# Expert blocks of a routed two-layer network: gathers three blocks ahead, two buffers each, first-layer weights split before the second layer

## The chip, the cores and the metric

The kernel runs on one core of one Trainium2 chip. The core has five engines that run side by side, each in the order of its own queue: TensorE (PE in the profile, with its weight loads as PEld), VectorE (DVE), ScalarE (ACT), GpSimd (POOL) and SyncE (SP, which here only issues DMAs). They wait for each other and for DMAs through semaphores. The metric is the device time of one execution in microseconds (us), given as the median of several runs.

## What is computed

The reference is an attention layer followed by a routed feed-forward network. Keys and values are averaged over groups of 8 positions (576 to 72), attention runs per batch (8) and head (8), and its output gives 8 x 576 = 4608 rows of 512 numbers. Each row then goes through one of 8 experts:

```python
logits = np.einsum('bsd,de->bse', x, w_gate)
local_gate = 1.0 / (1.0 + np.exp(-np.einsum('bsd,de->bse', x, w_local).squeeze(-1)))
...
        fresh_e = int(np.argmax(logits[b, s]))
        if s == 0 or local_gate[b, s] < 0.5:
            e = fresh_e
        else:
            e = prev_e if prev_e >= 0 else fresh_e
...
        h = np.maximum(x[b, s] @ w1[e], 0.0)
        out[b, s] = p[e] * (h @ w2[e])
```

Which expert a row uses is known only when the kernel has computed the logits. w1[e] is 512 x 1024 and w2[e] is 1024 x 512.

## The kernel before

The first part (attention, logits, choice of expert) writes the 4608 rows to a table in memory, `x_rows`, and for each expert a list of its rows. It ends in a small table `tab`, read with `entry`, that cuts the lists into **blocks** of up to 256 rows of one expert. A block with 128 rows or fewer is a **single** (`l1_one`), the others are **two-half blocks** (`l1_two`). Two plans written out by hand (`PLAN_B`, `PLAN_C`) set the order of the work up to block 0; then block 1 and the blocks from 2 on follow, the latter in `blocks(b)`, an unrolled chain of conditionals on registers.

Every product is made of three products with values split in a rounded upper part and its remainder: ScalarE writes the upper part, VectorE subtracts it from the original. So an expert's weights need four such pairs for w1 (`weights1`, `split1`, tiles w1h and w1l) and four for w2 (`weights2`, `split2`, w2h and w2l), from raw copies that SyncE has loaded, and each block's 256 rows need two (`x_split`). TensorE's first layer (lines 331 and 333) fills eight PSUM tiles one after the other; ScalarE and VectorE empty each with two operations apiece (lines 338, 339, 343, 344). Six PSUM tiles rotate there (hp, tp and rt). The second layer (line 352) makes the two output halves, half 1 first. `emit_scale` multiplies a half by its gate on VectorE into `ob`, and `emit_rows` scatters it to the output with an indirect DMA from GpSimd's queue.

In the kernel before, one block runs in this order: the first layer; `next_x`, which is the transposing of the next block's gathered rows (`x_turn`, line 319), the sums that give the list of rows to gather (`ids_sum`) and the two splits of the transposed rows; `fetch`, in which GpSimd issues eight indirect DMAs (`gather`, line 315) for the block after the next and SyncE loads another list; then `rest`: the second layer's half 1, its scaling and scatter, half 0, the splits of w1 and of w2 if the next block has another expert, and the scaling and scatter of half 0. There is one buffer each for the gathered rows (`xk`), the list (`idk`), the split rows (`xt`) and the outputs (`ob`). So that one DMA wait is taken at one place, GpSimd executes tiny operations that touch a buffer after its DMA: `seen_o` (line 1069) waits until the scatter from `ob` is done and then lets `emit_scale` write it; `seen_x` (line 1072) does the same for gathered rows; `emit_rows` copies its positions first (lines 1075 and 1076); `fetch` has two more (lines 1087 and 1088). `meta_shift` moves the positions and gates of three blocks along.

## Time and profile before

| | us |
|---|---|
| median of 3 runs (724.74 to 728.71) | 727.87 |
| profiled execution | 729.17 |
| its span, first to last instruction | 727.0 |
| blocks 1 to 20, TensorE (279.32 to 708.76) | 429.44 |
| from TensorE's last matmul to the end of the span | 18.24 |

Times in the rows are us from the start of the span. A timeline row gives start, duration, engine, line of the kernel, operation, destination and source; brackets give the idle time before it and what ended it. A name such as DVEq stands for an engine's instruction stream itself (a branch, say) and not for a computation. [...] Busy time is not progress: a matmul at half clock is busy for longer.

### The profile page before, as it was taken

What the parts mean: (1) busy time and instruction counts of PE and PEld (TensorE: products, weight loads), DVE (VectorE), ACT (ScalarE), POOL (GpSimd) and SP (SyncE); (2) the same over time, 40 slices, a digit from 0 to 9 for tenths busy, and PEclk for the clock granted to TensorE, in tenths of its full rate; (3) what the DMA queues carried; (4) which work ended last, traced back from release to release, by engine and by line L of the source; (5) the groups of instructions that cost most, each with busy time, mean ns of one, the idle gap of its engine ahead of it and who ended that gap; (6) DMA issues with size and microseconds to landing.
All of it is one profiled execution on the core that took longest, in us unless ns stands there. A gap on an engine that the chain in (4) does not pass through costs nothing. (4 is left out here: it accounts for less than half of the span.)

```text
span 727.0 us, 12051 instructions
## 1 busy us (share of the span) xinstructions
PE 633.5 (87%) x3588; PEld 534.7 (74%) x3588; DVE 454.3 (62%) x1061; ACT 273.1 (38%) x612; POOL 444.9 (61%) x652
## 2 busy tenths in 40 slices
PE   2868798787798999989999979799998996999990
PEld 1757687676686888778888768588877884888880
DVE  5557699887777743354569338478944486844450
ACT  1234354335354342232265126165622264422230
POOL 5165658675557543667556667676766766766553
PEclk9989899977679999999999989899999998899995
DMA  7988754744412127111117214426721136611111
GB/s 199 312 270 290 248 206 166 230 147 148 121 61 96 30 74 265 37 57 46 50 53 266 63 44 158 166 69 247 272 62 46 45 109 238 237 60 47 42 50 39
DMA packets 49443, 97.52 MB, mean 134 GB/s; under 512 B 22974, under 2 KB 22978, under 8 KB 49348
## 3 DMA queue, kind: packets, MB, share of 16 engines
q1 hardware_dynamic: 38820, 74.34, 30.6%
q0 software_dynamic: 10528, 22.08, 9.7%
q8 instruction: 39, 0.64, 0.4%
q14 instruction: 56, 0.46, 0.2%
HBM read 76.28 MB, written 22.21 MB: 135 GB/s over the span
## 5 line engine op out<-in xcount | busy, mean ns | idle before, releaser
L315 POOL DMA_INDIRECT kt<-x_rows,idk x168 | 185.1, 1102 | 48.8 <-issue 39.0
L331 PE MATMUL hp<-x,w1h 128*128 128x512 f32 x376 | 143.5, 419 | 7.4 <-ACT w1h L213 3.6
L352 PE MATMUL o_ps<-w2h,ht_h 128*128 128x512 f32 x312 | 122.6, 393 | 1.5 <-PEq L1141 1.5
L333 PE MATMUL hp<-x,w1l 128*128 128x256 f32 x376 | 111.1, 296 | 12.8 <-DVEq L1147 10.5
L352 PE MATMUL o_ps<-w2h,ht_l 128*128 128x512 f32 x312 | 121.7, 390 | 0.0
L352 PE MATMUL o_ps<-w2l,ht_h 128*128 128x512 f32 x312 | 121.6, 390 | 0.0
L331 PEld LDWEIGHTS hp<-x,w1h 128*128 128x128 f32 x376 | 75.4, 200 | 26.4 <-ACT w1h L213 4.1
L333 PEld LDWEIGHTS hp<-x,w1l 128*128 128x128 f32 x376 | 75.6, 201 | 17.3 <-DVEq L1147 12.3
L338 ACT COPY hs<-hp 128x256 f32<-128x256 f32 x94 | 34.8, 371 | 140.7 <-PE hp L333 140.5
L567 PE MATMUL op<-vaug,aT 128*128 128x148 f32 (+4 forms) x448 | 77.8, 340 | 2.1 <-ACT aT L377 1.8
L567 PEld LDWEIGHTS op<-vaug,aT 128*128 128x128 f32 (+1 forms) x448 | 69.4, 203 | 8.7 <-ACT aT L377 3.1
L339 DVE TENSOR_TENSOR hs<-hp,hs 128x256 f32<-128x256 f32 x94 | 39.4, 422 | 56.8 <-ACT hs L338 55.3
L352 PEld LDWEIGHTS o_ps<-w2h,ht_h 128*128 128x128 f32 x312 | 58.6, 188 | 14.7 <-ACT ht_h L966 2.5
L1066 DVE TENSOR_SCALAR ob<-o_ps,m_a 128x512 f32<-128x512 f32 x42 | 31.5, 749 | 59.3 <-PE o_ps L352 41.0
L343 ACT ACTIVATE ht_h<-hs 128x256 fp32r<-128x256 f32 x136 | 57.1, 420 | 30.1 <-DVE hs L339 30.1
L352 PEld LDWEIGHTS o_ps<-w2h,ht_l 128*128 128x128 f32 x312 | 58.5, 188 | 12.7
L352 PEld LDWEIGHTS o_ps<-w2l,ht_h 128*128 128x128 f32 x312 | 58.6, 188 | 11.5
L344 DVE SCALAR_TENSOR_TENSOR ht_l<-hs,ht_h 128x256 fp32r<-128x256 f32 x136 | 58.7, 432 | 5.9 <-ACT ht_h L343 5.8
L1077 POOL DMA_INDIRECT out<-ob,m_e x42 | 44.3, 1054 | 25.8 <-issue 25.8
L1069 POOL TENSOR_TENSOR ob<-zf 128x1 f32<-128x1 f32 x61 | 19.1, 313 | 54.0 <-DMA out<-ob,m_e 53.6
L383 POOL TENSOR_TENSOR t<-vt_in 128x512 f32<-128x512 f32 (+1 forms) x22 | 24.9, 1132 | 39.8 <-DMA vt_in<-in_v 39.4
L377 ACT COPY osb<-op 128x444 f32<-128x444 f32 (+2 forms) x56 | 26.5, 477 | 52.6 <-PE op L567 47.2
(261 smaller groups left out, 1184.2 us busy)
## 6 DMA issues: line engine op xcount, KB each, us to landing
raw<-in_moe_w SPq DMA_DIRECT2D x56, 512.0 KB
kk<-in_k SPq DMA_DIRECT2D x16, 576.0 KB
vt_in<-in_v SPq DMA_DIRECT2D x16, 512.0 KB
qt<-in_q SPq DMA_DIRECT2D x16, 512.0 KB
x_rows<-xs SPq DMA_DIRECT2D x16, 512.0 KB
kt<-x_rows,idk POOLq DMA_INDIRECT x168, 2.6
vt_in<-in_v SPq DMA_DIRECT2D x8, 256.0 KB
vt_in<-in_moe_w SPq DMA_DIRECT2D x4, 512.0 KB
```

What stands on the lines that cost most here:

```text
L315: nc.gpsimd.indirect_dma_start(out=xk[:, j, :], out_offset=None, in_=x_pc[0:4 * rows], in_offset=bass.IndirectOffsetOnAxis(ap=idk[:, j:j + ...
L331: nc.tensor.matmul(out=ps, lhsT=W1[0][:, kk, f * P:(f + 1) * P], rhs=xt[:, kk].rearrange("p i n -> p (i n)"), start=(kk == 0), stop=False, ...
L333: nc.tensor.matmul(out=ps[:, 0:2 * P], lhsT=W1[1][:, kk, f * P:(f + 1) * P], rhs=xt[:, kk, 0, :], start=False, stop=(kk == KD - 1), skip_g ...
L338: nc.scalar.copy(out=hb[:, 0, :], in_=ps[:, 2 * P:])
L339: nc.vector.tensor_tensor(out=hb[:, 1, :], in0=ps[:, 0:2 * P], in1=hb[:, 0, :], op=ALU.add)
L343: nc.scalar.activation(out=ht[0][:, f, :], in_=hb, func=AF.Relu)
L344: nc.vector.scalar_tensor_tensor(out=ht[1][:, f, :], in0=hb, scalar=0.0, in1=ht[0][:, f, :].bitcast(F32), op0=ALU.max, op1=ALU.subtract)
L352: nc.tensor.matmul(out=to[h], lhsT=ht[i][:, kk, h * P:(h + 1) * P], rhs=W2[j][:, kk, :], start=(n == 0), stop=(n == 3 * KF - 1))
L377: nc.scalar.copy(out=out, in_=in_)
L567: nc.tensor.matmul(out=out, lhsT=lhs, rhs=rhs if len(out.shape) == 3 else rhs.rearrange("p s x -> p (s x)"), start=all(x[0] != n for x in ...
L1066: nc.vector.tensor_scalar(out=ob[:, h, :], in0=o_ps[h], scalar1=m_a[:, h, 1:2], scalar2=None, op0=ALU.mult)
L1077: nc.gpsimd.indirect_dma_start(out=outv, out_offset=bass.IndirectOffsetOnAxis(ap=m_e[h][:, 0:1], axis=0), in_=ob[:, h, :], in_offset=None, ...
```

## The change

There are two buffers for gathered rows, the list of positions, split rows and outputs, and six small tiles for positions and gates, so that nothing is shifted. GpSimd's tiny operations are gone. The gather for block b + 3 is issued in block b, right after its first layer (`ahead`); two gathers are now in the plan ahead of block 1 (f2 and, new, f4). The next block's rows are transposed at the start of a block, and split in the first layer's course (after its tiles 3 and 5) or, in a single, ahead of it. The w1 splits stand ahead of the second layer; those of w2 stay behind it, under a second conditional.

```diff
--- before.py
+++ after.py
-M1:0 M1:1 M1:2 M1:3 i2:0 M1:4 M1:5 f0:0 f1:0 i3:0 f2:0 M1:6 M1:7 YR:0 M2:0 M2:1 M2:2 M2:3 Y1:0 M2:4 M2:5 Y0:0 M2:6 M2:7
+M1:0 M1:1 M1:2 M1:3 i2:0 M1:4 M1:5 f0:0 f1:0 i3:0 f2:0 M1:6 M1:7 YR:0 M2:0 M2:1 M2:2 M2:3 Y1:0 M2:4 M2:5 Y0:0 f3:0 i4:0 f4:0 M2:6 M2:7
...
-    m_a = route.tile([P, 2, 2], F32, name="m_a", bufs=1)
-    m_b = route.tile([P, 2, 2], F32, name="m_b", bufs=1)
-    m_i = route.tile([P, 2], I32, name="m_i", bufs=1)
-    m_c = route.tile([P, 2, 2], F32, name="m_c", bufs=1)
+    ms = [route.tile([P, 2, 2], F32, name=f"ms{i}", bufs=1) for i in range(NM)]
+    mi = [route.tile([P, 2], I32, name=f"mi{i}", bufs=1) for i in range(NM)]
...
-    idk = route.tile([P, TB], I32, name="idk", bufs=1)
+    idk = [route.tile([P, TB], I32, name=f"idk{i}", bufs=1) for i in range(2)]
...
-    def ids_sum():
+    def ids_sum(b):
         nc.vector.tensor_reduce(out=ids4, in_=idp.rearrange("p u j w -> p j w u"), axis=AX.X, op=ALU.add)
-        nc.vector.tensor_copy(out=idk, in_=ids4[:, :, 0])
+        nc.vector.tensor_copy(out=idk[b % 2], in_=ids4[:, :, 0])
...
-    def x_turn(js=slice(0, TB)):
-        nc.vector.transpose(out=xr_t.rearrange("p k (j t) -> p j k t", t=32)[:, js],
-                            in_=xk.rearrange("p j (k c) -> p j k c", c=32)[:, js])
+    def x_turn(b):
+        nc.vector.transpose(out=xr_t.rearrange("p k (j t) -> p j k t", t=32),
+                            in_=xk[b % 2].rearrange("p j (k c) -> p j k c", c=32))
...
-    def x_split(c2):
-        cs = slice(2 * c2, 2 * c2 + 2)
+    def x_split(b, c2):
+        xt, cs = xtb[b % 2], slice(2 * c2, 2 * c2 + 2)
...
+            elif op == "f3":
+                ids_sum(3)
+                meta(3)
+            elif op == "f4":
+                gather(3)
+            elif op == "i4":
+                ids_load(bass.ds(entry(4, 1, (EN.SP,), NU32 - TB), TB))
...
-        ob = sp.tile([P, 2, D], F32, name="ob")
+        ob = [sp.tile([P, 2, D], F32, name="ob0"), ld.tile([P, 2, D], F32, name="vt_in", bufs=3)]
...
-        def emit_rows(h):
-            nc.gpsimd.tensor_tensor(out=m_e[h], in0=m_i[:, h:h + 1], in1=zi, op=ALU.add)
-            nc.gpsimd.tensor_tensor(out=zf2[:, h:h + 1], in0=m_e[h].bitcast(F32), in1=ob[:, h, 0:1], op=ALU.mult)
...
-        def fetch(b):
-            nc.gpsimd.tensor_tensor(out=xk[:, :, 0:1], in0=idk.bitcast(F32).unsqueeze(2), in1=zf, op=ALU.mult)
-            nc.gpsimd.tensor_tensor(out=zf[:, 0, 0:1], in0=zf1, in1=zf1, op=ALU.subtract)
-            seen_o(1)
-            gather(js=range(0, 1))
-            seen_o(0)
-            gather(js=range(1, TB))
-            ids_load(bass.ds(entry(b + 3, 1, (EN.SP,), NU32 - TB), TB))
...
+    def ahead(b):
+        ids_sum(b + 3)
+        meta(b + 3)
+        gather(b + 3)
+        ids_load(bass.ds(entry(b + 4, 1, (EN.SP,), NU32 - TB), TB))
+
+    def l1_two(b):
+        for f in range(KF):
+            l1_pair(f, xtb[b % 2])
+            if f in (3, 5):
+                x_split(b + 1, (f - 3) // 2)
+
+    def single(b):
+        for c2 in range(2):
+            x_split(b + 1, c2)
+        l1_one(xtb[b % 2])
+
+    def rest(b, two):
+        chg = entry(b + 1, 2, (EN.Activation, EN.DVE, EN.Pool, EN.SP), 1)
+        nx = entry(b + 1, 3, (EN.SP,), E - 1)
+        with tc.If(chg > 0):
+            weights1(nx)
+        if two is None:
             l2(1)
...
-            with tc.If(single > 0):
+            with tc.If(two > 0):
                 l2(1)
-            emit_scale(1)
-            seen_x(0)
-            emit_rows(1)
+        emit_scale(b, 1)
+        emit_rows(b, 1)
         l2(0)
         with tc.If(chg > 0):
-            weights1(nx)
             weights2(nx)
-        emit_scale(0)
-        seen_o(1)
-        seen_x(1)
-        emit_rows(0)
...
-    emit_scale(0)
-    seen_o(1)
-    emit_rows(0)
-    l1_two()
-    next_x()
-    fetch(1)
+    emit_scale(0, 0)
+    emit_rows(0, 0)
+    x_turn(2)
+    l1_two(1)
+    ahead(1)
     rest(1, None)
...
             two = entry(b, 0, (EN.PE, EN.Activation, EN.DVE), 1)
+            x_turn(b + 1)
             with tc.If(two > 0) as both:
-                l1_two()
+                l1_two(b)
             with both.Else():
-                l1_one()
-            next_x()
-            fetch(b)
+                single(b)
+            ahead(b)
             rest(b, two)
```

The other edits follow from these: indices are passed along, and the tiles of the tiny operations are gone.

**VectorE at the end of a block.** Before, from the last operations of the positions to the next block's branch:

```order
L309 TENSOR_TENSOR picked<-ids_181,pickm 128x2x4x2
L311 TENSOR_REDUCE m_c<-picked 128x4
L1141 COMPARE_AND_BRANCH
L1141 UNCONDITIONAL_BRANCH x2
L1066 TENSOR_SCALAR ob<-o_ps_2475,m_a 128x512
L1147 COMPARE_AND_BRANCH
L214 TENSOR_TENSOR w1l<-raw_3001,w1h 128x1024 x4
L219 TENSOR_TENSOR w2l<-raw_3002,w2h 128x1024 x4
L1147 UNCONDITIONAL_BRANCH x2
L1066 TENSOR_SCALAR ob<-o_ps_2474,m_a 128x512
```

And now, from the last operation of the positions on:

```order
L311 CAST mi_186<-ms_180 128x2
L225 TENSOR_LOAD tab
L1123 COMPARE_AND_BRANCH
L215 TENSOR_TENSOR w1l<-raw_3020,w1h 128x1024 x4
L1123 UNCONDITIONAL_BRANCH x2
L1128 COMPARE_AND_BRANCH
L1128 UNCONDITIONAL_BRANCH x2
L1061 TENSOR_SCALAR vt_in<-o_ps_2472,ms_177 128x512
L1133 COMPARE_AND_BRANCH
L220 TENSOR_TENSOR w2l<-raw_3021,w2h 128x1024 x4
L1133 UNCONDITIONAL_BRANCH x2
L1061 TENSOR_SCALAR vt_in<-o_ps_2471,ms_177 128x512
```

The four w1 splits (w1l) moved from behind the scaling of half 1 to ahead of it, under a conditional of their own. The positions now end in `ms` and `mi`, and the output goes to one of two tiles (ob or vt_in, in turn).

**VectorE at the start of a two-half block.** Before, the emptying of the first layer's tiles stands right behind the branch:

```order
L1176 COMPARE_AND_BRANCH
L224 TENSOR_LOAD tab
L1178 COMPARE_AND_BRANCH
L339 TENSOR_TENSOR hs<-hp_2471,hs 128x256
L339 TENSOR_TENSOR hs<-hp_2472,hs 128x256
L344 SCALAR_TENSOR_TENSOR ht_l<-hs,ht_h 128x256
L339 TENSOR_TENSOR hs<-hp_2473,hs 128x256
```

And now:

```order
L1148 COMPARE_AND_BRANCH
L225 TENSOR_LOAD tab
L319 STREAM_TRANSPOSE qt<-kt 128x8x4x32
L1151 COMPARE_AND_BRANCH
L339 TENSOR_TENSOR hs<-hp_2468,hs 128x256
L339 TENSOR_TENSOR hs<-hp_2469,hs 128x256
L344 SCALAR_TENSOR_TENSOR ht_l<-hs,ht_h 128x256
L339 TENSOR_TENSOR hs<-hp_2470,hs 128x256
L344 SCALAR_TENSOR_TENSOR ht_l<-hs,ht_h 128x256
L339 TENSOR_TENSOR hs<-tp,hs 128x256
L344 SCALAR_TENSOR_TENSOR ht_l<-hs,ht_h 128x256
L325 TENSOR_TENSOR x_2192<-qt,x_2192 128x2x256
```

The transposing (L319) came to the head of the block, and the split of the next rows (L325) into the first layer.

**GpSimd, from the gathers to the end of the block.** Before, with the tiny operations and the first of the two scatters:

```order
L1087 TENSOR_TENSOR kt<-idk,zf 128x8
L1088 TENSOR_TENSOR zf<-zf_2462 128x1
L1069 TENSOR_TENSOR ob<-zf_2462 128x1
L315 DMA kt<-x_rows,idk 128x128
L1069 TENSOR_TENSOR ob<-zf_2462 128x1
L315 DMA kt<-x_rows,idk 128x128 x7
L224 TENSOR_LOAD tab
L1072 TENSOR_TENSOR zg<-kt 128x1
L1075 TENSOR_TENSOR m_e_2459<-m_i,zi 128x1
L1141 UNCONDITIONAL_BRANCH
L1076 TENSOR_TENSOR zf_2464<-m_e_2459,ob 128x1
L1077 DMA out<-ob,m_e_2459 4608x512
```

And now, with both scatters:

```order
L315 DMA kt<-x_rows,idk_190 128x128 x8
L225 TENSOR_LOAD tab
L1123 COMPARE_AND_BRANCH
L1123 UNCONDITIONAL_BRANCH x2
L1128 UNCONDITIONAL_BRANCH
L1064 DMA out<-vt_in,mi_185 4608x512
L1133 COMPARE_AND_BRANCH
L1133 UNCONDITIONAL_BRANCH x2
L1064 DMA out<-vt_in,mi_185 4608x512
```

Only the DMAs are left of GpSimd's work in a block. The list is one of two tiles in turn (idk_190 here, idk_191 in the next block).

## Rows read from the trace of the kernel before

**Rows 1.** The page's first part: busy us, share of the span and instructions of each engine.

```profile
PE 633.5 (87%) x3588; PEld 534.7 (74%) x3588; DVE 454.3 (62%) x1061; ACT 273.1 (38%) x612; POOL 444.9 (61%) x652
```

**Rows 2.** The windows view, one row a block, cut where TensorE's first matmul of a block begins. A row with about 113 PE instructions is a two-half block, one with about 57 a single; the last row runs from TensorE's last matmul to the end.

```profile
301.55:314.39 12.84, 12.23 (x57) 9.84 (x56) 5.61 (x13) 3.40 (x6) 6.92 (x13) 1.00 0.17 49
314.39:338.60 24.21, 22.29 (x114) 18.71 (x112) 11.86 (x29) 6.76 (x18) 17.89 (x30) 1.00 0.19 55
338.60:360.83 22.23, 22.23 (x113) 18.82 (x112) 11.16 (x28) 6.77 (x18) 12.79 (x22) 1.00 0.16 50
...
418.17:447.77 29.60, 24.82 (x113) 20.80 (x112) 15.74 (x33) 13.00 (x25) 19.23 (x30) 0.88 0.19 55
447.77:464.39 16.62, 12.39 (x58) 9.69 (x56) 9.77 (x13) 4.86 (x8) 10.67 (x15) 0.96 0.75 267
464.39:490.12 25.73, 24.37 (x113) 20.24 (x113) 16.82 (x39) 12.77 (x25) 18.94 (x29) 0.89 0.23 65
...
547.60:574.06 26.46, 24.02 (x114) 20.00 (x112) 12.02 (x30) 6.77 (x18) 19.10 (x31) 0.94 0.15 45
...
596.29:612.94 16.65, 12.41 (x58) 9.66 (x56) 10.47 (x17) 5.93 (x10) 11.10 (x16) 1.00 0.73 268
612.94:641.89 28.95, 26.67 (x112) 21.23 (x113) 21.34 (x40) 13.31 (x25) 22.05 (x29) 0.82 0.53 184
...
708.76:727.00 18.24, 0.00 (x0) 0.00 (x0) 0.75 (x1) 0.00 (x0) 6.70 (x13) 0.59 0.13 39
```

**Rows 3.** Timeline of TensorE: the five matmuls at the starts of blocks before which it had stood idle longest.

```profile
316.70 0.38 PE L333 MATMUL hp<-x,w1l 128*128 128x256 f32 x1 [1.92 <-DVEq L1147]
...
423.34 0.58 PE L333 MATMUL hp<-x,w1l 128*128 128x256 f32 x1 [4.78 <-DVEq L1147]
...
464.39 0.76 PE L331 MATMUL hp<-x,w1h 128*128 128x512 f32 x1 [3.62 <-DVE x L325]
...
550.42 0.38 PE L333 MATMUL hp<-x,w1l 128*128 128x256 f32 x1 [2.44 <-DVEq L1147]
...
612.94 0.58 PE L331 MATMUL hp<-x,w1h 128*128 128x512 f32 x1 [3.63 <-ACT w1h L213]
```

**Rows 4.** Timeline of GpSimd and VectorE around two of these: the block from 418.17, and the single from 447.77.

```profile
416.87 0.18 POOL L1069 TENSOR_TENSOR ob<-zf 128x1 f32<-128x1 f32 x1 [3.18 <-DMA out<-ob,m_e]
...
420.76 1.01 POOL L1077 DMA_INDIRECT out<-ob,m_e  x1 [3.15 <-issue]
...
422.48 0.75 DVE L1066 TENSOR_SCALAR ob<-o_ps,m_a 128x512 f32<-128x512 f32 x1 [4.43 <-POOL ob L1069]
...
461.56 1.25 DVE L319 STREAM_TRANSPOSE qt<-kt 128x1024 f32<-128x1024 f32 x1 [5.44 <-DMA out<-ob,m_e]
```

**Rows 5.** The windows view of the two layers of the block from 574.06, the last before a single at whose start the weights change: first layer, second layer.

```profile
574.06:585.35 11.29, 11.29 (x66) 9.79 (x64) 5.71 (x14) 4.51 (x13) 6.86 (x13) 1.00 0.16 54
585.35:596.29 10.94, 10.94 (x50) 9.01 (x49) 9.30 (x19) 8.53 (x12) 6.07 (x8) 1.00 0.26 79
```

**Rows 6.** Groups of instructions from 279.32 to 708.76, shapes kept apart: count, busy us, mean ns of one, and what ended the idle time before them.

```profile
L344 DVE SCALAR_TENSOR_TENSOR ht_l<-hs,ht_h 128x256 fp32r<-128x256 f32 x120 | 50.4, 420 | 2.9 <-ACT ht_h L343 2.8
...
L325 DVE TENSOR_TENSOR x<-qt,x 128x512 fp32r<-128x512 f32 x40 | 25.9, 690 | 7.1 <-ACT x L324 7.1
...
L319 DVE STREAM_TRANSPOSE qt<-kt 128x1024 f32<-128x1024 f32 x20 | 24.9, 1244 | 13.7 <-DMA out<-ob,m_e 10.1 <-DMA kt<-x_rows,idk 1.8 <-issue 0.3
L213 ACT CAST w1h<-raw 128x1024 fp32r<-128x1024 f32 x24 | 23.4, 1046 | 0.6 <-ACT x L324 0.3
...
L324 ACT CAST x<-qt 128x512 fp32r<-128x512 f32 x40 | 22.9, 619 | 50.5 <-DVE qt L319 50.5
...
L305 DVE TENSOR_REDUCE ids<-idp 128x16 f32<-128x80 f32 x20 | 5.1, 253 | 0.0
```

**Rows 7.** Timeline of VectorE from the end of the first layer at 585.35: the last emptying operation, the four w1 splits and the four w2 splits.

```profile
586.92 0.43 DVE L344 SCALAR_TENSOR_TENSOR ht_l<-hs,ht_h 128x256 fp32r<-128x256 f32 x1 [0.15 <-ACT ht_h L343]
...
592.35 4.67 DVE L214 TENSOR_TENSOR w1l<-raw,w1h 128x1024 fp32r<-128x1024 f32 x4
596.94 4.62 DVE L219 TENSOR_TENSOR w2l<-raw,w2h 128x1024 fp32r<-128x1024 f32 x4
```

**Rows 8.** The gathers of the whole trace (ns shortest, median and longest, first and last start), and the time from issue to landing of the scatters to the output.

```profile
L315 POOL DMA_INDIRECT kt<-x_rows,idk x168: 940/947/1970, 266.9 to 712.2; - x168
...
DMA to landing us min/median/max: 2.1/2.8/7.2
```

**Rows 9.** Timeline of the last block: the list on VectorE, then on GpSimd the first and last gather, and the two scatters with the wait between them.

```profile
701.25 0.17 DVE L306 CAST idk<-ids 128x8 int32<-128x8 f32 x1
...
703.27 1.00 POOL L315 DMA_INDIRECT kt<-x_rows,idk  x1
...
712.18 0.95 POOL L315 DMA_INDIRECT kt<-x_rows,idk  x1 [0.30 <-issue]
...
714.32 1.04 POOL L1077 DMA_INDIRECT out<-ob,m_e  x1 [0.57 <-issue]
716.80 0.18 POOL L1069 TENSOR_TENSOR ob<-zf 128x1 f32<-128x1 f32 x1 [1.44 <-DMA out<-ob,m_e]
...
718.11 1.01 POOL L1077 DMA_INDIRECT out<-ob,m_e  x1 [0.57 <-issue]
```

**Rows 10.** Timeline of TensorE in a single: the first matmul behind the conditional that skips half 1.

```profile
308.86 0.47 PE L352 MATMUL o_ps<-w2h,ht_h 128*128 128x512 f32 x1 [0.30 <-PEq L1141]
```

More of the change, by code (lines that the diff above doesn't have):

```diff
@@ L37 @@
 NS = 2
+NM = 6
 VCH = [list(range((P * c) // G, (P * c + P - 1) // G + 1)) for c in range(4)] + [[H - 1, H - 1]]
@@ L302, in ids_load, with meta, gather @@
                               ids[u][:, r, :].rearrange("t j w -> t (j w)").unsqueeze(0).broadcast_to([4, 32, 2 * TB]))
-    def ids_sum():
+    def ids_sum(b):
         nc.vector.tensor_reduce(out=ids4, in_=idp.rearrange("p u j w -> p j w u"), axis=AX.X, op=ALU.add)
-        nc.vector.tensor_copy(out=idk, in_=ids4[:, :, 0])
-    def meta():
+        nc.vector.tensor_copy(out=idk[b % 2], in_=ids4[:, :, 0])
+    def meta(b):
         nc.vector.tensor_tensor(out=picked.rearrange("p h w j -> p h j w")[:, :, 0:4, :],
                                 in0=ids4.rearrange("p (h j) w -> p h j w", h=2), in1=pickm, op=ALU.mult)
-        nc.vector.tensor_reduce(out=m_c, in_=picked, axis=AX.X, op=ALU.add)
-    def gather(rows=NT + 1, js=range(TB)):
-        for j in js:
-            nc.gpsimd.indirect_dma_start(out=xk[:, j, :], out_offset=None, in_=x_pc[0:4 * rows],
-                                         in_offset=bass.IndirectOffsetOnAxis(ap=idk[:, j:j + 1], axis=0))
-    def x_turn(js=slice(0, TB)):
-        nc.vector.transpose(out=xr_t.rearrange("p k (j t) -> p j k t", t=32)[:, js],
-                            in_=xk.rearrange("p j (k c) -> p j k c", c=32)[:, js])
-    def x_split(c2):
-        cs = slice(2 * c2, 2 * c2 + 2)
+        nc.vector.tensor_reduce(out=ms[b % NM], in_=picked, axis=AX.X, op=ALU.add)
+        nc.vector.tensor_copy(out=mi[b % NM], in_=ms[b % NM][:, :, 0])
+    def gather(b):
+        for j in range(TB):
+            nc.gpsimd.indirect_dma_start(out=xk[b % 2][:, j, :], out_offset=None, in_=x_pc,
+                                         in_offset=bass.IndirectOffsetOnAxis(ap=idk[b % 2][:, j:j + 1], axis=0))
+    def x_turn(b):
[3 more added lines that the diff above has]
+        xt, cs = xtb[b % 2], slice(2 * c2, 2 * c2 + 2)
         nc.scalar.copy(out=xt[:, cs, 0, :], in_=xr_t[:, cs, :])
@@ L847, in do @@
             elif op == "ma":
-                rows_meta(m_a, NS - 1)
-                nc.vector.tensor_copy(out=m_i, in_=idrs[NS - 1])
+                rows_meta(0, NS - 1)
             elif op == "L1":
@@ L860, in do @@
                 h = n % 2
-                nc.scalar.activation(out=ob[:, h, :], in_=o_ps[h], func=AF.Copy, scale=idms[n // 2][:, h, 1:2])
+                nc.scalar.activation(out=ob[1][:, h, :], in_=o_ps[h], func=AF.Copy, scale=idms[n // 2][:, h, 1:2])
             elif op == "so":
@@ L900, in do @@
             elif op == "e1":
-                emit_scale(1)
-                emit_rows(1)
+                emit_scale(0, 1)
+                emit_rows(0, 1)
             elif op == "f0":
-                rows_meta(m_b, NS)
+                rows_meta(1, NS)
             elif op == "f1":
-                ids_sum()
-                meta()
+                ids_sum(2)
+                meta(2)
             elif op == "f2":
-                xk = ld.tile([P, TB, PC], F32, name="kt", bufs=2)
+                xk.update({i: ld.tile([P, TB, PC], F32, name="kt", bufs=2) for i in range(2)})
                 xr_t = ld.tile([P, KD, 2 * P], F32, name="qt", bufs=4)
-                gather()
+                gather(2)
+            elif op == "f3":
[5 more added lines that the diff above has]
+                ids_load(bass.ds(entry(4, 1, (EN.SP,), NU32 - TB), TB))
             elif op == "i3":
@@ L950, in l1_pair, with l1_one @@
                 l1_l(f)
[L952 removed]
+        def l1_one(xt):
             for f in range(2):
```

72 lines of the change are left out of this document (18 added, 54 removed).

## Prediction

> **What bounds the kernel now.** I read the page's first part first: TensorE is busy for 633.5 of 727.0 us, far above VectorE with 454.3 and GpSimd with 444.9 [rows 1]. So the question is where TensorE stands still, and whether the change reaches those places. The windows view by block answers the first half [rows 2]. An undisturbed two-half block takes 22.23 us (the row from 338.60), an undisturbed single 12.84 (from 301.55). Against these, seven blocks are long: 24.21 (1.98 too much), 29.60 (7.37), 25.73 (3.50), 26.46 (4.23) and 28.95 (6.72) among the two-half ones, and the two singles with 16.62 (3.78) and 16.65 (3.81). Together that is 31.4 us. All seven are a single or the block behind one.
>
> Their starts show the cause. TensorE stood idle for 1.92, 4.78, 3.62, 2.44 and 3.63 us before the matmuls named, and what ended it was VectorE's instruction stream, the split of x, or the split of w1 [rows 3]. The worst one can be followed backwards: at 422.48 VectorE starts a scaling for which it had waited 4.43 us, on GpSimd's tiny operation on `ob`, which GpSimd could reach only after a scatter issued at 420.76; in the single before it GpSimd had waited 3.18 us for an earlier scatter to land [rows 4]. The conditional around the splits stands behind that scaling in VectorE's queue, and the next first layer waits for it even when nothing is split. In the single from 447.77 the transposing itself waited 5.44 us for a scatter, seen through GpSimd's queue [rows 4]. So GpSimd, with its landings waited for in order, falls behind in a single's 12.84 us, and holds VectorE, which holds TensorE. The clock adds to it: behind the idle 4.78 and 3.63 us the granted clock fell, to a mean of 0.88 and 0.82 in those blocks, where it is 1.00 in an undisturbed one [rows 2]. The other part is the tail: 18.24 us in which TensorE does nothing [rows 2].
>
> **The change, part by part.** The terms are made against the profiled execution, 729.17 us (span 727.0 and 2.17 around it), which is 1.30 above the median of 727.87.
>
> *Tiny operations and shared buffers go.* VectorE's scaling no longer waits for GpSimd but for a scatter two blocks back; the transposing waits for a gather issued two blocks earlier. At 2.8 us median and 7.2 us longest landing [rows 8] both are over long before. The waits of rows 4 thus go, and with them the excess of the five two-half blocks and of the two singles: -31.4 us as the most, if nothing new takes their place. What is late next is the subject of the next two parts.
>
> *w1 split ahead of the second layer.* I count from the end of a first layer, at 585.35 in rows 7. VectorE's last emptying ends at +2.0. The positions take five small operations of about 0.2 to 0.25 us (the first is 0.253 [rows 6]), so the splits begin at +3.3 instead of +7.0 and, at 4.67 us for four [rows 7], end at +8.0 instead of +11.7. ScalarE's upper parts, 4 x 1.046 us [rows 6], run ahead of them. The second layer lasts 10.94 us [rows 5], so the next first layer finds w1 ready with 2.9 us to spare: cost nothing, covered by the second layer. Then scaling 0.75, w2 splits 4.62, scaling 0.75, transposing 1.24: VectorE begins to empty the next first layer at +15.4. TensorE has by then filled three of its six tiles (11.29 us for eight [rows 5], 1.41 each, from +10.94) and would stop only at +19.4. Nothing again, in a two-half block.
>
> *Singles behind a change (from 447.77 and 596.29).* ScalarE now has the two splits of the next rows, 2 x 0.619 [rows 6], ahead of the first ReLU, and these wait for the transposing that ends at +15.4: free at +16.6. TensorE's first layer of a single ends near +16.4, and its transposes need the ReLU: 0.6 us late each, 1.2 in all.
>
> *The one single at whose end the weights change again (from 596.29).* Its second layer is 5.5 us (half of 10.94). VectorE copies the second operand until about 4.5 us behind the first layer, does the positions until 5.6, and splits until about 10.3; TensorE wants the last w1 chunk near 9.0. About 1.3 us of waiting; then VectorE, late by the w2 splits, frees the first of the six tiles about 0.3 late and delivers its last operands about 0.7 late, since it needs near 1 us a tile to catch up. So 2.3 us, where the trace has 6.72 + 3.81 at this place. Bounds: from 0 (all behind the catch-up) to those 10.5 again.
>
> *Splits of x in the first layer.* Per two-half block VectorE has 2 x 0.69 and ScalarE 2 x 0.62 more between the emptyings, but no longer behind the layer; a tile leaves 1.41 us, of which the emptying takes 2 x 0.42 [rows 6]. Nothing, as 1.38 us are caught up over eight tiles with 0.57 us free on each.
>
> *More gathers in the plan, and SyncE.* GpSimd issues eight gathers more ahead of block 1, at 0.947 us and 0.30 between [rows 8, 9] about 10 us; what waits behind them in its queue are only block 0's scatters, which nobody needs before block 2. On SyncE the first raw load of the weights comes behind another list load, several blocks ahead of its first use. Nothing.
>
> *Tail.* The last list comes 1.2 us earlier without the transposing ahead of it; then 1.85 us of tiny operations lie between the list and the first gather (701.42 to 703.27), 0.4 remain; the gathers lose 0.36 us of another; before each scatter 0.6 to 0.7 us go [rows 9]. The wait of one scatter for the other to land stays (the order of writes to `out` is kept). 1.2 + 1.45 + 0.36 + 0.63 + 0.74 = 4.4 us.
>
> *One conditional more per block.* On TensorE it shows as a branch more between the layers. The only branch that costs TensorE anything in the trace is the skip in a single, 0.30 us [rows 10]; at the border of two-half blocks, where three branches and a load stand, nothing is lost, or 22.23 would not repeat. So between 0 and 20 x 0.30 = 6 us; I take 0, the nearer row. [...]
>
> Sum: 729.17 - 31.4 + 1.2 + 2.3 - 4.4 = 696.9; at the median's level, 1.30 lower, 695.5 us. The cases of this forecast lie between 690 (nothing new costs anything: 729.17 - 31.4 - 4.4 - 1.3 = 692, and 2 for the smaller gaps that I did not count) and 703 (6 for the branches).
>
> **The rivals.**
>
> *VectorE becomes the bound where the weights change.* There are six changes (24 splits of w1 at four each [rows 6]), each with 9.3 us of VectorE's time, and the clock falls behind an idle stretch. For it: behind an idle 2.44 us the block lost 4.23, so 1.8 more by the clock [rows 2, 3]. Against it: today the w1 splits end at +11.7, 0.7 us behind the start of the next block, and that single still takes no time at its start; now they end 3.7 us earlier. Price: five further changes at 2 us, 10 us: 706, with up to 713 if the clock follows in some.
>
> *The first layer goes on waiting for the conditional.* If the release comes late for another reason than the scatters (the stream itself, a load of a register), the stalls stay and only the tail is won: 727.87 - 4.4 = 723.5. For it: the releaser is named as VectorE's stream. Against it: the stream is behind the scaling in every one of these.
>
> *Slower: GpSimd's queue sets the pace.* Per block it needs 8 x (0.95 + 0.30) for the gathers, 2 x 1.6 for the scatters [rows 9] and the landing between them, since the second scatter still waits for the first: 16.0 us with the median landing, below the mean block of 429.44 / 20 = 21.5. With four of the gathers at their longest of 1.97, as beside the splits, and the longest landing of 7.2 [rows 8] it is 24.5. Then GpSimd is the bound: the transposing stands at the head of VectorE's queue, and a gather that lands more than 8.5 us (six tiles) into the block before its own stops TensorE in each block. Between the two ends, at 23 us, that gives 23 x 20 + 279.3 + 18.2 = 757.5 us. Against it: weights load in 6 of 20 blocks only, and a whole block of slack lies in between. It decides once the mean need is above 21.5 us.
>
> **How the numbers follow.** The forecast has 0.78 (690 to 703), VectorE at the changes 0.12 (703 to 713), the surviving stalls 0.05, GpSimd's pace 0.03, and 0.02 are left for a change that does nothing. The range of 8 in 10 is 690 to 707. A difference under 0.5% (3.6 us) can't be told from none here. Faster by more: 0.78 + 0.12 + 0.05 = 0.95; slower: 0.03; the same: 0.02.
>
> **What would show it.** Right: in the windows by block, 22.2 us for every two-half block and 12.8 to 13.5 for the singles; no idle time of TensorE ended by VectorE's stream; gathers while the second layer runs, at up to twice their length beside the splits, with nobody waiting; one block of about 24 us, the one behind the single with a change; a tail near 14 us. Wrong: idle time on the transposing that a gather's landing ends (GpSimd's pace); a first layer that waits for w1l in more than one block, or one that stops at its seventh tile (VectorE); a gap of 0.3 us between the layers in every block (branches).

## The result, and the profile after

The changed kernel takes 693.50 us (median of 4 runs, 693.06 to 694.76), the kernel before 728.15 beside it: a ratio of 0.9536 (95% interval 0.9504 to 0.9568). Forecast were 695.5 us and a range of 690 to 707. In a second set of runs (e8 below) the ratio was 0.9560; in a third, on another chip (e12), it was 1.0025, which the last section tells of. The profiled execution has a span of 691.4 us; its busy times, to be held against [rows 1]:

```profile
PE 621.9 (90%) x3588; PEld 526.4 (76%) x3588; DVE 448.8 (65%) x1026; ACT 272.4 (39%) x612; POOL 381.9 (55%) x431
```

TensorE has the same 3588 matmuls, in less time, because the granted clock no longer falls (in the twenty blocks 395.73 us busy at a mean of 1.00, against 406.30 at 0.97 before; from 423.30 to 425.00 of the kernel before, at 0.50, matmuls of line 331 into hp took 0.63 us, against a mean of 0.42 of that group); GpSimd has 221 instructions fewer. The windows by block (length in us, busy time of PE, PEld, DVE, ACT and POOL with the number of instructions begun, TensorE's granted clock as a share of full speed, DMA share, GB/s) answer to [rows 2]; the first row is all twenty blocks, the last one the tail:

```profile
275.99:675.54 399.55, 395.73 (x1961) 330.88 (x1959) 247.16 (x498) 163.72 (x348) 212.21 (x205) 1.00 0.37 126
...
311.06:333.29 22.23, 22.23 (x113) 18.81 (x112) 10.82 (x26) 6.63 (x18) 13.14 (x14) 1.00 0.17 49
412.87:435.11 22.24, 22.24 (x114) 18.81 (x112) 17.67 (x33) 13.70 (x25) 13.42 (x13) 1.00 0.27 84
435.11:448.77 13.66, 12.52 (x57) 9.69 (x56) 8.37 (x14) 4.25 (x7) 5.73 (x6) 1.00 0.80 296
448.77:471.01 22.24, 22.24 (x114) 18.81 (x112) 17.44 (x32) 13.70 (x25) 16.24 (x15) 1.00 0.29 85
528.35:550.59 22.24, 22.24 (x114) 18.80 (x112) 10.83 (x26) 6.63 (x18) 13.11 (x14) 1.00 0.17 45
572.82:586.14 13.32, 12.47 (x57) 9.69 (x56) 10.92 (x16) 9.29 (x13) 5.90 (x6) 1.00 0.82 298
586.14:608.67 22.53, 22.53 (x113) 18.80 (x112) 17.02 (x33) 8.94 (x21) 14.26 (x13) 1.00 0.63 222
...
675.54:691.40 15.86, 0.00 (x0) 0.00 (x0) 0.75 (x1) 0.00 (x0) 3.07 (x4) 0.66 0.09 31
```

The seven long blocks of before read 22.23, 22.24, 13.66, 22.24, 22.24, 13.32 and 22.53 here. Of 31.4 us of excess, 0.82 + 0.48 + 0.30 = 1.60 are left. The blocks went from 429.44 to 399.55 us (-29.89), the tail from 18.24 to 15.86 (-2.38). Block 1 begins at 275.99 instead of 279.32 (-3.33), for which the prediction had no term. The two groups of VectorE on which the waits stood (count, busy us, mean ns, idle before them) show where the time had been:

```profile
L319 DVE STREAM_TRANSPOSE qt<-kt 128x1024 f32<-128x1024 f32 x20 | 24.8, 1242 | 2.1 <-DMA kt<-x_rows,idk 0.5 <-issue 0.5
...
L1061 DVE TENSOR_SCALAR ob<-o_ps,ms 128x512 f32<-128x512 f32 x20 | 15.0, 748 | 47.0 <-PE o_ps L352 45.6 <-DVEq L1123 1.4
```

The transposing waits 2.1 us in all instead of 13.7 [rows 6], and the scaling waits for TensorE's result, not for GpSimd.

### The profile page after: what moved, and what is told of

It reads as the page before. It is cut to its first block, busy times and chain, and to the rows that moved or that the text cites. A ratio compares the mean times of both kernels' runs of the same rounds, so it can differ in the third digit from the quotient of the medians.

```text
span 691.4 us, 11897 instructions
## 1 busy us (share of the span) xinstructions
PE 621.9 (90%) x3588; PEld 526.4 (76%) x3588; DVE 448.8 (65%) x1026; ACT 272.4 (39%) x612; POOL 381.9 (55%) x431
## 3 DMA queue, kind: packets, MB, share of 16 engines
q0 software_dynamic: 10784, 22.60, 10.3%
## 5 line engine op out<-in xcount | busy, mean ns | idle before, releaser
L315 POOL DMA_INDIRECT kt<-x_rows,idk x176 | 180.7, 1027 | 113.8 <-DVE picked L308 64.7
L331 PE MATMUL hp<-x,w1h 128*128 128x512 f32 x376 | 135.9, 402 | 0.1
L333 PE MATMUL hp<-x,w1l 128*128 128x256 f32 x376 | 106.2, 282 | 0.0
L338 ACT COPY hs<-hp 128x256 f32<-128x256 f32 x94 | 34.8, 370 | 147.4 <-PE hp L333 146.9
L331 PEld LDWEIGHTS hp<-x,w1h 128*128 128x128 f32 x376 | 71.3, 190 | 17.9 <-DVE hs L339 0.6
L333 PEld LDWEIGHTS hp<-x,w1l 128*128 128x128 f32 x376 | 71.7, 191 | 0.9 <-DVE w1l L215 0.3
L1061 DVE TENSOR_SCALAR ob<-o_ps,ms 128x512 f32<-128x512 f32 x22 | 16.5, 748 | 51.7 <-PE o_ps L352 50.3
L1064 POOL DMA_INDIRECT out<-ob,mi x22 | 23.0, 1047 | 46.1 <-DVE mi L311 10.8
L703 POOL DMA_INDIRECT ids<-pm,pos x36 | 35.7, 991 | 19.3 <-DVE pos L700 9.4
```

Of the source, the lines that this page charges most:

```text
L315: nc.gpsimd.indirect_dma_start(out=xk[b % 2][:, j, :], out_offset=None, in_=x_pc, in_offset=bass.IndirectOffsetOnAxis(ap=idk[b % 2][:, j:j ...
L331: nc.tensor.matmul(out=ps, lhsT=W1[0][:, kk, f * P:(f + 1) * P], rhs=xt[:, kk].rearrange("p i n -> p (i n)"), start=(kk == 0), stop=False, ...
L333: nc.tensor.matmul(out=ps[:, 0:2 * P], lhsT=W1[1][:, kk, f * P:(f + 1) * P], rhs=xt[:, kk, 0, :], start=False, stop=(kk == KD - 1), skip_g ...
L338: nc.scalar.copy(out=hb[:, 0, :], in_=ps[:, 2 * P:])
L703: nc.gpsimd.indirect_dma_start(out=ids[u % 4].rearrange("t m w -> (t m) w"), out_offset=bass.IndirectOffsetOnAxis(ap=pos[:, u:u + 1], axis=0),
```

## The experiments

The table puts all runs together. The last three columns are from each kernel's own profile, cut like the rows above: where block 1 begins, how long the twenty blocks take, and the tail behind TensorE's last matmul. e1 to e4, e9 and e10 ran on one chip, e5 to e8 on a second, e11 and e12 on a third; on which chip the first pair ran is not on record.

| kernel | us | before beside it | ratio (95% interval) | block 1 at | blocks | tail |
|---|---|---|---|---|---|---|
| before | 728.15 | | | 279.32 | 429.44 | 18.24 |
| changed | 693.50 | 728.15 | 0.9536 (0.9504 to 0.9568) | 275.99 | 399.55 | 15.86 |
| e1 w1 late | 701.46 | 727.09 | 0.9649 (0.9599 to 0.9699) | 278.81 | 405.68 | 16.31 |
| e2 before, w1 first | 715.38 | 727.09 | 0.9849 (0.9803 to 0.9895) | 279.54 | 415.42 | 20.64 |
| e3 before, two outputs | 715.47 | 727.09 | 0.9861 (0.9815 to 0.9907) | 280.01 | 415.01 | 17.98 |
| e4 x late | 702.97 | 727.09 | 0.9678 (0.9628 to 0.9728) | 278.25 | 404.02 | 18.53 |
| e5 one output | 696.57 | 727.49 | 0.9575 (0.9513 to 0.9638) | 277.47 | 399.95 | 15.68 |
| e6 interleaved | 694.04 | 727.49 | 0.9547 (0.9494 to 0.9600) | 276.91 | 399.67 | 13.12 |
| e7 no dead gathers | 688.10 | 727.49 | 0.9465 (0.9411 to 0.9520) | 277.63 | 399.50 | 8.47 |
| e8 changed again | 694.45 | 727.49 | 0.9560 (0.9494 to 0.9626) | 275.75 | 399.65 | 15.20 |
| e9 two ahead, x late | 710.40 | 727.27 | 0.9759 (0.9703 to 0.9815) | 276.61 | 414.39 | 17.20 |
| e10 before, e2 + e3 | 714.05 | 727.27 | 0.9820 (0.9772 to 0.9867) | 278.01 | 413.61 | 18.18 |
| e11 e5 + e7 | 732.44 | 740.88 | 0.9882 (0.9835 to 0.9929) | 278.73 | 441.11 | 8.66 |
| e12 changed, third chip | 741.21 | 740.88 | 1.0025 (0.9999 to 1.0050) | 279.77 | 440.57 | 16.96 |

### Two ways of cutting the chain: e2, e3, e10

My theory: the three stalls on VectorE's stream (1.98 + 7.37 + 4.23 us of excess) come from a chain, scatter landing, GpSimd's queue, VectorE's scaling, the conditional behind it, the next first layer. e2 cuts it behind the scaling, e3 ahead of it, both in the kernel before.

```diff
 e2, in rest(j, single) of the kernel before
         meta_shift()
+        with tc.If(chg > 0):
+            weights1(nx)
...
         with tc.If(chg > 0):
-            weights1(nx)
             weights2(nx)
```

> The kernel before with one part of the change alone: the w1 splits, with a conditional of their own, ahead of the second layer; GpSimd's waits stay. If the first layer waits for the conditional only because it stands behind the late scaling, the stalls of the three two-half blocks with VectorE's stream as releaser go (1.98 + 7.37 + 4.23 = 13.6 us) and those of the two places where a scatter holds the transposing stay (17.8): about 714.5 us (709 to 718). Rival one (VectorE is late anyway, and the stall moves to the emptying of the tiles): 722 to 728. Rival two (the order alone carries the gain): below 702.

```diff
 e3, in the kernel before
-        ob = sp.tile([P, 2, D], F32, name="ob")
+        ob = [sp.tile([P, 2, D], F32, name="ob0"), ld.tile([P, 2, D], F32, name="vt_in", bufs=3)]
...
-            seen_o(1)
-            gather(js=range(0, 1))
-            seen_o(0)
-            gather(js=range(1, TB))
+            gather()
```

> The kernel before with a second output buffer and without GpSimd's two waits for scatters ahead of the gathers; positions, rows and split order as before. If the chain scatter landing, GpSimd, VectorE's scaling, first layer is the cause, the three stalls on VectorE's stream go (13.6 us), and of the 17.8 at the other two places the part that came from gathers issued late: 703 to 716 us. Rival (the gathers must be issued a block or more earlier, since GpSimd's need in a single is above 12.84 us whatever waits): 720 to 728, with the transposing waiting for gathers.

Both came out at 715.4 and 715.5 us, inside what the theory gave. In e2 the block that had 29.60 us is an undisturbed one (windows view, then the timeline of the next single, where GpSimd's last gather, the transposing and the next first layer follow each other):

```profile
416.41:438.65 22.24, 22.24 (x114) 18.83 (x113) 15.36 (x32) 12.53 (x25) 17.25 (x25) 1.00 0.20 58
```

```profile
450.57 0.94 POOL L315 DMA_INDIRECT kt<-x_rows,idk  x1 [0.30 <-issue]
...
453.34 1.25 DVE L319 STREAM_TRANSPOSE qt<-kt 128x1024 f32<-128x1024 f32 x1 [6.33 <-DMA kt<-x_rows,idk]
...
456.16 0.60 PE L331 MATMUL hp<-x,w1h 128*128 128x512 f32 x1 [4.51 <-DVE x L325]
```

What stays is the other kind of stall: the rows are gathered too late behind a change of weights. e3 shows the same at the same place (timeline):

```profile
453.67 1.25 DVE L319 STREAM_TRANSPOSE qt<-kt 128x1024 f32<-128x1024 f32 x1 [6.30 <-DMA out<-ob,m_e]
...
456.49 0.77 PE L331 MATMUL hp<-x,w1h 128*128 128x512 f32 x1 [4.43 <-DVE x L325]
```

The two rows name different releasers for one wait; a landing in GpSimd's queue stands for whatever came last there. e3 takes two of GpSimd's waits away together with adding the buffer, so it does not tell which of the two helped. To see whether the two cuts remove the same time, e10 has both edits:

> The kernel before with the edits of e2 and e3 together: w1 split ahead of the second layer, and two output buffers without GpSimd's waits ahead of the gathers. Each alone gave about 12 us. If both remove the same three stalls on VectorE's stream (one chain, cut at two places), the second adds nothing: 713 to 717 us. If they remove different time, the gains add up: 701 to 706 us.

It took 714.05 us; its blocks, 413.61, are 1.8 and 1.4 us shorter than those of e2 and e3. One chain, cut twice: the second cut gains almost nothing. The rival in which the gains add up (701 to 706) is out.

### What removed the stalls on the rows: e4, e9

```diff
 e4, in the changed kernel
     def l1_two(b):
         for f in range(KF):
             l1_pair(f, xtb[b % 2])
-            if f in (3, 5):
-                x_split(b + 1, (f - 3) // 2)
...
     def single(b):
-        for c2 in range(2):
-            x_split(b + 1, c2)
         l1_one(xtb[b % 2])
...
-            x_turn(b + 1)
...
+            x_turn(b + 1)
+            for c2 in range(2):
+                x_split(b + 1, c2)
             ahead(b)
```

> The changed kernel with the transposing and the two splits of the next rows back behind the first layer, ahead of the positions. If buffers and scatter waits are the cause: the rows have landed long before, VectorE's w1 splits begin about 2.6 us later, which costs only in the single whose end changes the weights (about 3 us), while the ReLU behind a change is earlier by 0.5 to 0.8 in two singles: 692 to 698 us. Rival (having the rows split during the first layer is what removed the waits on x): the two places with 17.8 us in the kernel before lose again: 702 to 711 us.

The time, 702.97, lies where the rival had it, but not for its reason. Of the 9.5 us above the changed kernel, 4.5 are in the blocks, 2.7 in the tail and 2.3 ahead of block 1. No wait on x came back; the singles behind a change are even 12.88 instead of 13.66 and 13.32. What the blocks lose lies in one of them, which waits for w1l and then runs at a lower granted clock, 0.88 where the block at this place in the changed kernel has 1.00 (windows view; then the timeline of its first waits):

```profile
587.45:615.41 27.96, 26.01 (x114) 20.96 (x112) 20.57 (x35) 12.12 (x24) 17.11 (x15) 0.88 0.56 198
```

```profile
588.65 0.39 PE L333 MATMUL hp<-x,w1l 128*128 128x256 f32 x1 [0.81 <-DVE w1l L215]
```

I had priced this place at 3 us; it is 5.4 (27.96 against 22.53). The tail is 2.7 us longer, since the last list comes behind the transposing again. So the early split of the rows is worth its 4.5 us in the blocks through VectorE's queue, not through the rows. e9 then takes away the third block of distance:

```diff
 e9, on top of e4 (and without the plan's second gather ahead)
     def ahead(b):
-        ids_sum(b + 3)
-        meta(b + 3)
-        gather(b + 3)
+        ids_sum(b + 2)
+        meta(b + 2)
+        gather(b + 2)
```

> The version e4 (changed kernel, the next rows transposed and split behind the first layer) with the gathers issued two blocks ahead instead of three, so the same distance from gather to transposing as in the kernel before, but with two row buffers, none of GpSimd's tiny operations and w1 split first. What is open is what removed the two stalls on the rows at the changes of weights, 4.5 and 2.7 us of idle TensorE that both e2 and e3 still have. Theory one (GpSimd runs late behind a single, and only an earlier gather covers that): both stalls return, with the transposing waiting for gathers, 5 to 11 us above e4's 703.0: 707 to 714 us. Theory two (the tiny operations and their waits made GpSimd late; without them the distance of before is enough): 701 to 705 us.

710.40 us, with the blocks 10.4 us longer than e4's: theory one. In the single behind a change (timeline) the last gather is issued at 442.70, the transposing can begin at 448.30, 5.6 us later, beside the raw loads of the weights (the DMA share of this single is 0.86), and TensorE waits:

```profile
442.70 0.94 POOL L315 DMA_INDIRECT kt<-x_rows,idk  x1 [0.30 <-issue]
...
448.30 1.25 DVE L319 STREAM_TRANSPOSE qt<-kt 128x1024 f32<-128x1024 f32 x1 [4.30 <-DMA out<-ob,mi]
...
451.07 0.47 PE L331 MATMUL hp<-x,w1h 128*128 128x512 f32 x1 [2.42 <-DVE x L325]
```

The releaser named for the transposing is a scatter, which it does not read; at the second place the row names a gather, issued last at 586.39, 5.4 us before the transposing (timeline):

```profile
591.80 1.25 DVE L319 STREAM_TRANSPOSE qt<-kt 128x1024 f32<-128x1024 f32 x1 [3.85 <-DMA kt<-x_rows,idk]
```

So for these two places, without any tiny operation left, it is the distance between gather and use that decides.

### What the other parts are worth: e1, e5

```diff
 e1, in rest(b, two) of the changed kernel
-        with tc.If(chg > 0):
-            weights1(nx)
         if two is None:
...
         with tc.If(chg > 0):
+            weights1(nx)
             weights2(nx)
```

> The changed kernel with the w1 splits back behind the second layer, next to the w2 splits. Theory (the gain comes from the second set of buffers and from scaling that no longer waits for GpSimd): VectorE starts the w1 splits some 3.4 us later, which a two-half block covers; only the single at whose end the weights change, and the singles behind a change, lose 2 to 5 us each: 695 to 704 us. Rival (splitting w1 first carries the gain): the stalls at the first layer on VectorE's stream come back, 15 us or more are lost: above 708 us.

701.46 us, as the theory had it; the blocks lose 6.1 us: 6.4 in the two singles behind a change (16.83 and 16.56 instead of 13.66 and 13.32), of which the block behind the second gives back 0.3. The transposing comes behind both sets of splits in a row there, and the first ReLU is late (timeline of TensorE in the first of them):

```profile
446.14 0.66 PE L959 MATMUL hp<-ident,hs 128*128 128x128 f32 x4 [2.58 <-ACT hs L956]
```

```diff
 e5, in the changed kernel: emit_scale and emit_rows use ob[0] in every block
-ob[b % 2]
+ob[0]
```

> The changed kernel with a single output buffer again, everything else as changed; VectorE's scaling then waits for the landing of the scatter of the block before, but through the DMA itself and not through an operation in GpSimd's queue. Theory one (what held VectorE was GpSimd's queue, with gathers, landings and tiny operations in order): the scatters of a block are landed some 20 us behind the end of its first layer, the next scaling comes later than that even in a single, so nothing is lost: 692 to 697 us. Theory two (the second output buffer itself is what removed the three stalls on VectorE's stream): they return, about 13 us: 703 to 710 us.

The median is 696.57, 2.1 us above e8's on the same chip, which the intervals don't separate; the blocks take 399.95 us against e8's 399.65. With one buffer no scaling of VectorE waits for a DMA in e5; in e2, which also has one buffer and w1 split first, seven still wait for GpSimd's tiny operation (views of VectorE's waits, e5 and e2: us in total, times, longest):

```profile
DVE ob L1061 <- PE o_ps L352: 82.3, 24, 4.7
```

```profile
DVE ob L1066 <- POOL ob L1069: 7.8, 7, 2.3
```

So in the changed kernel the second output buffer is not needed. That the direct wait alone would have removed the three stalls is not shown: e5 also splits w1 first, and e2 shows that this order keeps late scalings from TensorE. One buffer with the direct wait and w1 split last was not run.

### The tail, and a version that beats both: e6, e7

```diff
 e6, in the changed kernel
-        gather(b + 3)
+        gather(b + 3, range(4))
...
         emit_rows(b, 1)
+        gather(b + 3, range(4, TB))
         l2(0)
```

> The changed kernel with the last four of each block's eight gathers issued behind the scatter of half 1, so that its landing passes beside them. If the tail is GpSimd's queue (eight gathers, scatter, 3.4 us of landing, scatter), the last scatter is issued at about 677.5 instead of 681.6, 3 to 4 us are won there and nothing elsewhere: 689 to 691 us. Rival (the landing of a scatter beside gathers takes longer, so that the wait only moves): 692 to 694.5 us.

The median, 694.04, missed the 689 to 691 that I expected. It lies where the rival had it, but not for its reason: the second scatter has no wait of its own left, it stands 0.30 us behind the last gather. In the profile the tail is 2.1 us shorter than e8's; that is less than the runs can tell from nothing (timeline of GpSimd, the two last scatters):

```profile
673.20 1.02 POOL L1064 DMA_INDIRECT out<-ob,mi  x1 [0.30 <-issue]
...
679.54 1.02 POOL L1064 DMA_INDIRECT out<-ob,mi  x1 [0.30 <-issue]
```

```diff
 e7, in the changed kernel (left is the number of blocks in a register of GpSimd)
     def ahead(b):
...
-        gather(b + 3)
+        if b < 2:
+            gather(b + 3)
+        else:
+            with tc.If(left > b + 3):
+                gather(b + 3)
```

> The changed kernel with the gathers of a block under a conditional of GpSimd alone, so that none are issued for the last three rounds of the loop, whose blocks don't exist. If the tail is GpSimd's queue, the last scatter of half 1 goes out when its scaling is done and that of half 0 about 5 us earlier than now (676.3 against 681.6): 687.5 to 690 us. Rival (the conditional costs GpSimd or others more than 0.25 us a block, or the tail is bound by the landing): 691.5 to 696 us.

688.10 us: theory one. The last scatter starts 0.27 us behind its scaling, and the tail is 8.47 us instead of 15.20 (windows view):

```profile
677.13:685.60 8.47, 0.00 (x0) 0.00 (x0) 0.75 (x1) 0.00 (x0) 0.98 (x1) 0.65 0.12 41
```

On that chip it stands 6.3 us below the changed kernel; their intervals still touch. e11 (e5 and e7 together) and e12 were meant to part them:

> The edits of e7 (no gathers for blocks that don't exist) and e5 (one output buffer) together on the changed kernel. If both readings stand (the tail is GpSimd's queue; the second buffer is not needed once the waits don't pass GpSimd), the time is e7's: 686 to 690.5 us, with a tail of 8 to 10 us. If the single buffer costs what e5's median hints at (2 us above the changed kernel beside it), 689.5 to 693 us.

> The changed kernel beside e11, in five rounds, so that the two can be told apart: 692.5 to 696 us, expert blocks 399.6 us, a tail of 15 to 16 us, and block 1 starting anywhere between 275.5 and 280 us.

They do: 732.44 against 741.21 us, ratios whose intervals (0.9835 to 0.9929, and 0.9999 to 1.0050) lie apart, with tails of 8.66 and 16.96 us. But neither time is near what was expected; see the last section.

### The start of block 1: e8

> The changed kernel itself once more, beside the three above, for the spread of what lies ahead of the first expert block. That part was 3.3 us shorter in the changed kernel's profile than in that of the kernel before, which the prediction has no term for. If this is spread of the attention part, block 1 starts anywhere between 276 and 280 us here, and the time is 692 to 698 us; if the changed plan made it, at 276.0 plus or minus 0.7, and the time is 692.5 to 694.5 us.

e8 gave 694.45 us, and block 1 began at 275.75. In the profiles other than those of e11 and e12 the kernels with the changed plan have it between 275.75 and 278.81, those with the old one (before, e2, e3, e9, e10) between 276.61 and 280.01. The two overlap, so the 3.33 us of the first pair of profiles are mostly spread of the attention part; whether some 1 us of it belongs to the change stays open.

## Why the prediction was right, point by point

- **The seven long blocks (-31.4).** Right: all are gone, and e2, e3, e9 and e10 show the two mechanisms behind them. What the prediction put together as one cause is two: the chain through GpSimd, worth 14 us, which either earlier w1 splits (e2) or a second output buffer with two of GpSimd's waits taken out (e3) cuts; and the late rows at two changes, which gathers a block earlier remove.
- **ReLU late behind a change (+1.2).** Measured 0.82 + 0.48 = 1.30. In the single from 435.11 (timeline) ScalarE does the two splits, then the ReLUs, and TensorE waits for them:

```profile
439.87 1.14 ACT L324 CAST x<-qt 128x512 fp32r<-128x512 f32 x2 [3.46 <-DVE qt L319]
...
440.92 1.07 ACT L956 ACTIVATE hs<-hp 128x512 f32<-128x512 f32 x2
441.56 0.66 PE L959 MATMUL hp<-ident,hs 128*128 128x128 f32 x4 [0.85 <-ACT hs L956]
```

- **The single at whose end the weights change again (+2.3).** The term was too large: the block behind it loses 0.30 us. The failing step is "splits until about 10.3", against a need near 9.0. Its positions were done near 4.1 us behind the first layer's end (about 578.4), not 5.6, and the splits ended at 587.49, 9.1 us behind it. The 0.3 and 0.7 for tiles and operands did not show.
- **w1 splits at no cost.** In the block from 550.59, 3.35 to 7.98 us behind the first layer against 3.3 to 8.0 forecast; nothing waited. The order is worth 6.1 us by e1.
- **GpSimd's pace.** Gathers beside the splits did take up to 1.97 us, against a median of 0.945 over all, and one scatter waited 6.20 for the other, with nobody behind it in need (timeline of GpSimd):

```profile
567.60 1.95 POOL L315 DMA_INDIRECT kt<-x_rows,idk  x1 [0.30 <-issue]
...
583.75 1.22 POOL L1064 DMA_INDIRECT out<-vt_in,mi  x1 [6.20 <-issue]
```

  The rival was wrong because the block of distance absorbs it; e9, without that block, has blocks 10.4 us longer than e4's.
- **The tail (-4.4).** Measured -2.4, in e8 -3.0. The timeline of VectorE and GpSimd answers to [rows 9]:

```profile
666.71 0.17 DVE L305 CAST idk<-ids 128x8 int32<-128x8 f32 x1
...
667.15 0.98 POOL L315 DMA_INDIRECT kt<-x_rows,idk  x1 [7.48 <-DVE picked L308]
...
675.94 0.94 POOL L315 DMA_INDIRECT kt<-x_rows,idk  x1 [0.30 <-issue]
677.19 1.02 POOL L1064 DMA_INDIRECT out<-ob,mi  x1 [0.30 <-issue]
681.62 1.01 POOL L1064 DMA_INDIRECT out<-ob,mi  x1 [3.40 <-issue]
```

  From the end of the first layer to the first gather it was 2.72 us instead of 5.62, 2.90 less where 2.65 were forecast; the gathers lost 0.12 (0.36 forecast), and the first scatter came 0.89 sooner behind the last gather (0.63). The step that failed is the 0.74 for the second scatter: the tiny operations went, but in this block it is 4.43 us from one scatter to the other against 3.79 before, 0.64 more. And the end comes 9.78 us behind the last scatter against 8.89, which the prediction held to be the same; why stays open. 2.90 + 0.12 + 0.89 - 0.64 - 0.89 = 2.38. In the other blocks the 0.74 did come; see the last section.
- **One conditional more (0 of up to 6 us).** Nothing here: 22.23 us repeats in the two-half blocks as before, and the branch in a single still costs the 0.30 of [rows 10]. The 6 us would have led to 701.5 at the median's level; the 703 of the prediction is at the profiled execution's.

The sum: blocks -29.9 instead of -27.9, tail -2.4 instead of -4.4. Two errors of 2 us cancel, by luck, so that the terms still come to 696.9 for the profiled execution. It took 693.06: of the other 3.8 us, 3.33 are block 1's earlier start and 0.5 lie outside the span (1.7 us instead of 2.17), and no term had either.

## What to carry to other kernels

Where a queue passes a landing on to another engine by small operations, look at what that engine then waits for: here VectorE's scaling waited for GpSimd's tiny operation eight times, for up to 4.43 us [rows 4]. Moving work ahead of the wait or taking the wait out of the queue may each take the whole stall (e2 and e3: blocks 14.0 and 14.4 us shorter), and the second then gains next to nothing (e10: 1.8 and 1.4 us more); a second buffer may then not be needed (e5: blocks of 399.95 us against 399.65). For rows that are gathered beside bulk loads, count the distance from the slowest landing: in the kernel before, the five gathers issued from 595.9 to 603.9, in the single with a DMA share of 0.73, landed after 6.8 to 7.4 us, those in the block from 338.60, with 0.16, after 2.5 to 2.6. And time a change on more than one chip: here a gain of some 34 us in two sets of runs was none on a third chip.
